# Row-half products in turns, one tile for the q of two heads, and other numbers in the planner of a linear-attention and MoE kernel

## The chip, the cores and the metric

One core of a Trainium2 chip runs the whole kernel. The metric is device time in microseconds (us), the median of the runs shown below. TensorE (PE) multiplies; its weight loads have rows of their own (PEld). VectorE (DVE) and ScalarE (ACT) do the elementwise work, GpSimd (POOL) a reduction over partitions, SyncE (SP) issues the DMAs.

## The reference

```python
def phi(x):
    proj = np.einsum('bhsd,df->bhsf', x, w_phi)
    proj = proj - np.max(np.abs(proj), axis=-1, keepdims=True)
    return np.concatenate([np.exp(proj), np.exp(-proj)], axis=-1)
q_p, k_p = (phi(q), phi(k))                      # q, k, v: 8 batches, 8 heads, 576 tokens, 64
kv = np.einsum('bhsf,bhsd->bhfd', k_p, v)        # w_phi: 64 x 128
z = np.sum(k_p, axis=2)
num = np.einsum('bhsf,bhfd->bhsd', q_p, kv)
den = np.einsum('bhsf,bhf->bhs', q_p, z)[..., None] + 1e-06
x = (num / den).transpose(0, 2, 1, 3).reshape(4608, 512)
out = ((x @ w_a) * (x @ w_b)) @ w_out            # 512 x 1536, 512 x 1536, 1536 x 512
```

## The kernel before

The heads are worked on in 32 pairs, i = 4 * batch + pr. For a pair `k_load` brings k and v of 512 of the 576 keys; the last 64 keys of two pairs share the tiles of `rest_load`: the first pair's lie in partitions 0 to 63, the second's in 64 to 127. `features` projects keys (tile pk), takes the largest absolute value (m), subtracts it (kd) and forms both exponentials (ke). `kv_add` (L288) multiplies them with v, which carries a column of ones, into the pair's sum kvps: for 512 keys in four chunks with 128 rows, and for the last 64 keys by `rest_add` with 64 rows, one pair at its own turn. `k_finish` copies kvps, transposes it (pt) and keeps the result as kvh and kvl.

On the query side `q_project` multiplies q with w_phi (tile pq, 288 tokens at a time, two heads, two halves), ACT copies the result (p), POOL finds the largest absolute value (mb), DVE subtracts it (L371), ACT forms both exponentials (qe) and `q_side` multiplies them with kv (tile pn).

Numbers are float32. Where a product is not "plain", each operand is split by `split` (L156 to L163) into a rounded high part in fp32r (ACT or DVE) and the rest (DVE), and three products of the parts stand for one of float32. The first pairs stay plain: PLAIN_K, PLAIN_Q and PLAIN_NUM are 5, PLAIN_KV is 7. A plain `q_project` (L342) loads q of two heads as one tile of 128 partitions and multiplies 64 rows at a time. The other kind loads each head's q twice, one copy over the other (four DMAs, two tiles of 128 partitions), and makes of it a tile qs that has the high part in the upper 64 rows and the rest in the lower (L355); wh and wl hold w_phi's parts in both halves, so that two products with 128 rows (L360) cover one head and one half of the tokens.

While attention runs, blocks of the first third of the MoE (`moe_block`, 512 tokens each, tiles pa, pb, po, L661 and L682) are put between its turns. When attention ends, the last of these blocks and two more passes with fewer products (L756, L861, L968) follow.

PSUM has eight banks here: two for ps_moe ("moe"), and in ps_att five for the tag "att" (pk, pq, pn) and one for "kvacc" (kvps and pt; in batch 0 these two use ps_moe).

The order on each engine is not that of the code: `plan` builds the program once, runs a list scheduler over it with a cost for each instruction (`Work`, the time in `LANDING` after which a DMA's data is taken to be there) and a count of the free buffers, and the second build is chained in that order. On an engine the earliest instruction of the code that is ready goes first.

Of the kernel before, what the change touches and what calls it, by code (L numbers as in the profile page):

```python
# [22 lines left out]
P = 128  # L23
# [8 lines left out]
REST_ADD_TURNS = (6, 7)  # L32
KV_TURNS = (7, 8)
PROJECT_TURNS = (0, 3, 3)
Q_TURNS, Q_STEP, QB, PB, Q32 = (4, 6, 10), 3, 2, 2, 2
# [8 lines left out]
PLAIN_K, PLAIN_Q, PLAIN_KV, PLAIN_NUM = 5, 5, 7, 5  # L44
# [23 lines left out]
def tile_kernel(ctx, tc, qT, km, kr, vm, vr, w_phi, w_a, w_b, w_out, out):  # L68
# [95 lines left out]

    def stack(hi_lo, src, eng_hi, eng_lo):

        copy(eng_hi, hi_lo, src)
        eng_lo.tensor_tensor(hi_lo[D:], src[D:], hi_lo[D:], op=ALU.subtract)
# [85 lines left out]
    def k_chunks(b, pr, c0, a1, a2, ps, consts, st):  # L254
# [6 lines left out]
        if c0 == 0:  # L261
            pool, tag, bufs = spare(b, ps)
            st["kv_ps", b, pr] = pool.tile([P, 2, 2 * F], F32, tag=tag, bufs=bufs, name=f"kvps_{u}")
            st["kv_left", b, pr] = NFULL + 1
        for c in range(2):
            kv_add(b, pr, [v_[:, c0 + c] for v_ in st["v", b, pr]], [e_[:, 2 * c : 2 * c + 2] for e_ in es], st)
# [14 lines left out]
    def kv_add(b, pr, vs, es, st):  # L281

        left = st["kv_left", b, pr] = st["kv_left", b, pr] - 1
        for j in range(2):
            parts = products(vs, es)
            for n_, (v_, e_) in enumerate(parts):
# [5 lines left out]
                    start=(left == NFULL and j == 0 and n_ == 0),  # L292
                    stop=(left == 0 and n_ == len(parts) - 1),
                    skip_group_check=True,
                )

    def spare(b, ps):

        return (ps_moe, "moe", 2) if b == 0 else (ps, "kvacc", 1)

    def k_finish(b, pr, a1, a2, ps, consts, st):
# [6 lines left out]
        pool, tag, bufs = spare(b, ps)  # L308
# [13 lines left out]
    def q_project(b, pr, a1, a2, ps, consts, st):  # L322
# [11 lines left out]
        if plain:  # L334
            q32 = a2.tile([P, S], F32, tag="q32", bufs=Q32, name=f"q32_{u}")
            nc.sync.dma_start(q32, qT[b, 2 * pr : 2 * pr + 2].rearrange("j d s -> (j d) s"))
            yield
            for i, tok in enumerate(toks):
                pq = [ps.tile([P, 512], F32, tag="att", name=f"pq_{u}_{j}_{i}") for j in range(2)]
# [1098 lines left out]
```

## Time and profile before

| | us |
|---|---|
| median of 3 runs | 1223.03 (1222.47 to 1224.77) |
| the profiled execution, its own time | 1223.91 |
| its span, first to last instruction | 1221.8 |
| PE busy | 1184.5 (97%), 6237 instructions |
| DVE busy | 1036.7 (85%), 1730 instructions |
| ACT busy | 740.0 (61%), 1388 instructions |
| POOL busy | 149.2 (12%) |

2.1 us of the execution lie outside its span, and the median lies 0.9 us under the profiled execution. A busy PE is an engine with a product in flight: a product of 256 columns has a row of 0.28 us, and the next one starts after about 0.12. So the rate of the engine is read from start to start, not from durations. A float32 product shows as two records. The last product of attention (L390) starts at 584.2 us of the span, the last of the first third of the MoE (L682) at 674.1.

### The profile page before, as it was taken

How to read it: one execution, taken by the hardware profiler on the slowest of the kernel's cores; microseconds unless marked ns; L12 is line 12 of the kernel's file. 1: busy time of each engine (PE TensorE's matmuls, PEld its weight loads, DVE VectorE, ACT ScalarE, POOL GpSimd, SP SyncE). 2: the span in 40 equal slices, each digit the busy share in tenths (PEclk: the TensorE clock that was granted, in tenths of full speed). 3: DMA queues.
4: the chain of work that ended last, by engine and by line, in shares of the span. 5: the costliest groups of instructions: out<-in, count | busy, mean ns of one | idle time of the engine just before them, and what ended most of it. 6: DMA issues, size and time to landing. Idle time of an engine off the chain costs nothing.

```text
span 1221.8 us, 17963 instructions
## 1 busy us (share of the span) xinstructions
PE 1184.5 (97%) x6237; PEld 981.5 (80%) x6237; DVE 1036.7 (85%) x1730; ACT 740.0 (61%) x1388; POOL 149.2 (12%) x68
## 2 busy tenths in 40 slices
PE   7997999999999999999989999999999999999998
PEld 4566888888888888888768988788877788888887
DVE  7999999998999899988576867888877687969686
ACT  5868898897888988887344533444434243534332
POOL 3232232223223213211000000000000000000000
PEclk9998999999999999999999999999999999999999
DMA  8654363455545445436762332837498634241322
GB/s 241 211 148 126 109 184 112 144 155 143 158 112 167 138 133 163 113 102 210 263 228 86 113 121 72 273 123 264 136 366 298 216 91 148 80 138 53 129 83 74
DMA packets 132922, 190.15 MB, mean 156 GB/s; under 512 B 35104, under 2 KB 64160, under 8 KB 132832
## 3 DMA queue, kind: packets, MB, share of 16 engines
q1 hardware_dynamic: 132832, 189.01, 49.4%
q8 instruction: 49, 0.80, 0.3%
q14 instruction: 41, 0.34, 0.1%
HBM read 126.73 MB, written 62.23 MB: 155 GB/s over the span
## 4 chain that ended last, share of the span: by engine, by line
PE 66%; DVE 17%; DMA 8%; issue 5%; ACT 2%; SPq 1%; POOL 0%; DVEq 0%; POOLq 0%; ACTq 0%
PE paa L756 7%; PE pba L756 7%; PE po L968 6%; PE kvps L288 6%; PE po L682 6%; PE pa L661 5%; PE pn L390 5%; PE pb L661 5%; PE poa L861 4%; PE pbc L756 3%; PE pac L756 3%; PE pk L232 2%; DMA o<-part 2%; PE poc L861 2%; PE pbb L756 2%
## 5 line engine op out<-in xcount | busy, mean ns | idle before, releaser
L370 POOL PARTITION_ALL_REDUCE mb<-p x64 | 149.0, 2372 | 408.0 <-ACT p L361 347.1
L163 DVE TENSOR_TENSOR qel<-qe,qeh 128x1152 fp32r<-128x1152 f32 x54 | 72.9, 1350 | 1.8 <-ACT qeh L156 1.5
L163 DVE TENSOR_TENSOR kel<-ke,keh 128x1024 fp32r<-128x1024 f32 x50 | 63.9, 1278 | 1.3 <-ACT keh L156 1.1
L371 DVE TENSOR_TENSOR p<-p,mb 128x576 f32<-128x576 f32 x64 | 61.3, 958 | 4.3 <-POOL mb L370 4.1
L156 ACT CAST qeh<-qe 128x1152 fp32r<-128x1152 f32 x54 | 62.8, 1163 | 0.1
L661 PE MATMUL pb<-xh,w_b_h 128*128 128x512 f32 x144 | 57.0, 396 | 3.2 <-DVE h L666 3.2
L968 PE MATMUL po<-hh,w_o_h 128*128 128x512 f32 x144 | 56.3, 393 | 3.0 <-DVE o L974 1.4
L682 PE MATMUL po<-hl,w_o_h 128*128 128x512 f32 x144 | 57.2, 397 | 1.2 <-DVE hl L163 1.1
L661 PE MATMUL pa<-xh,w_a_h 128*128 128x512 f32 x144 | 58.1, 403 | 0.0
L661 PE MATMUL pa<-xl,w_a_h 128*128 128x512 f32 x144 | 57.5, 399 | 0.0
L661 PE MATMUL pa<-xh,w_a_l 128*128 128x512 f32 x144 | 57.3, 398 | 0.0
L661 PE MATMUL pb<-xh,w_b_l 128*128 128x512 f32 x144 | 57.2, 397 | 0.0
L661 PE MATMUL pb<-xl,w_b_h 128*128 128x512 f32 x144 | 57.2, 397 | 0.0
L968 PE MATMUL po<-hl,w_o_h 128*128 128x512 f32 x144 | 56.3, 391 | 0.8 <-DVE hl L163 0.8
L682 PE MATMUL po<-hh,w_o_h 128*128 128x512 f32 x144 | 56.4, 395 | 0.5 <-ACT hh L156 0.5
L288 PE MATMUL kvps<-keh,vaug 128*65 128x256 f32 x200 | 56.1, 281 | 0.7 <-DVE kvl L318 0.7
L682 PE MATMUL po<-hh,w_o_l 128*128 128x512 f32 x144 | 56.7, 396 | 0.0
L288 PE MATMUL kvps<-kel,vaug 128*65 128x256 f32 x200 | 56.0, 280 | 0.6 <-DVE kel L163 0.6
L968 PE MATMUL po<-hh,w_o_l 128*128 128x512 f32 x144 | 56.1, 390 | 0.0
L244 ACT ACTIVATE ke<-kd 128x512 f32<-128x512 f32 x64 | 40.5, 633 | 25.4 <-DVE kd L236 25.3
L288 PE MATMUL kvps<-keh,vl 128*64 128x256 f32 x200 | 55.9, 279 | 0.0
L391 ACT COPY xn<-pn 65x288 f32<-65x288 f32 x128 | 48.8, 396 | 10.3 <-PE pn L390 9.1
(347 smaller groups left out, 3839.9 us busy)
## 6 DMA issues: line engine op xcount, KB each, us to landing
x<-xnorm SPq DMA_DIRECT2D x32, 512.0 KB
o<-part SPq DMA_DIRECT2D x61, 256.0 KB
q<-in_qT SPq DMA_DIRECT2D x108, 144.0 KB
xun<-xn SPq DMA_DIRECT2D x64, 146.2 KB
xnorm<-x SPq DMA_DIRECT2D x36, 256.0 KB
part<-o SPq DMA_DIRECT2D x18, 512.0 KB
part<-o SPq DMA_DIRECT2D x36, 256.0 KB
k<-in_km SPq DMA_DIRECT2D x32, 256.0 KB
```

The costliest lines, as they stand in the source:

```text
L156: eng.copy(dst, src)
L163: eng_lo.tensor_tensor(lo, src, hi, op=ALU.subtract)
L288: nc.tensor.matmul(st["kv_ps", b, pr][:width, j], v_[:, j, :width], e_[:, j], start=(left == NFULL and j == 0 and n_ == 0), stop=(left == ...
L370: nc.gpsimd.partition_all_reduce(mb, p32, P, bass_isa.ReduceOp.absmax)
L371: engine("q_sub", b).tensor_tensor(p32, p32, mb, op=ALU.subtract)
L390: nc.tensor.matmul(pn[: D + 1, :HALF], kv_[:, 2 * j + s, :], e_[:, s, tok], **at)
L391: nc.scalar.copy(xn[: D + 1, tok], pn[: D + 1, :HALF])
L661: nc.tensor.matmul(acc, w[:, cc * P : (cc + 1) * P], x, start=(k == 0), stop=(k == 3 * NCC - 1))
L682: nc.tensor.matmul(acc, w[:, cc * P : (cc + 1) * P], h, start=(k == 0), stop=(k == 3 * NFS[p] - 1))
L756: nc.tensor.matmul(accs[to][i], w_, x_, skip_group_check=True, **at)
L861: nc.tensor.matmul(accs[to][m], w_, x_, skip_group_check=True, **flags)
L968: nc.tensor.matmul(acc[key], w[:, cc * P : (cc + 1) * P], h[:, tok], skip_group_check=True, **n_)
```

## The change

1. `rest_add` now handles the last 64 keys of two pairs in one step. Its products stand in turns: one with rows 0 to 63 for the first pair, one with rows 64 to 127 for the second. For this two kvps tiles live at once: "kvacc" gets two banks, "att" four, and pt moves to "att" (in batch 0 to ps_moe).
2. Every `q_project` loads q of two heads as one tile (one DMA), and splits it whole (qh, ql). The products have 64 rows, in turns over the two heads: three for a head and a half where there were two with 128 rows. `stack` is gone.
3. One more pair is plain: PLAIN_K, PLAIN_Q, PLAIN_NUM 6, PLAIN_KV 8.
4. In the planner a product with 64 rows has a partner on the other half. The two are taken together, PE stays with products of the same number of rows for up to 40 places of the code, a change of rows costs 88 ns, float32 products are priced anew, the first product of a tile in "att" waits until the inputs of all of that tile's products are there, and `LANDING` has later and more times.

```diff
-REST_ADD_TURNS = (6, 7)
+REST_ADD_TURN = 6
-Q_TURNS, Q_STEP, QB, PB, Q32 = (4, 6, 10), 3, 2, 2, 2
+Q_TURNS, Q_STEP, QB, PB, Q32 = (4, 6, 10), 3, 1, 2, 2
-PLAIN_K, PLAIN_Q, PLAIN_KV, PLAIN_NUM = 5, 5, 7, 5
+PLAIN_K, PLAIN_Q, PLAIN_KV, PLAIN_NUM = 6, 6, 8, 6
-        ps = c.enter_context(tc.tile_pool(name="ps_att", bufs=5, space=PSUM))
+        ps = c.enter_context(tc.tile_pool(name="ps_att", bufs=4, space=PSUM))
...
-    def rest_add(b, pr, st):
-        rows = slice(pr % 2 * REST, (pr % 2 + 1) * REST)
-        kv_add(b, pr, [v_[rows] for v_ in st["rv", b, pr // 2]], [e_[rows] for e_ in st["re", b, pr // 2]], st)
+    def rest_add(b, g, ps, st):
+        vs, es = st["rv", b, g], st["re", b, g]
+        parts = products(vs, es)
+        first = [kv_sums(b, 2 * g + i, ps, st) for i in range(2)]
+        for j in range(2):
+            for n_, (v_, e_) in enumerate(parts):
+                width = D if n_ == 2 else D + 1
+                for i in range(2):
+                    rows, pr = slice(i * REST, (i + 1) * REST), 2 * g + i
+                    nc.tensor.matmul(
+                        st["kv_ps", b, pr][:width, j],
+                        v_[rows, j, :width],
+                        e_[rows, j],
...
+            st["kv_ps", b, pr] = ps.tile([P, 2, 2 * F], F32, tag="kvacc", bufs=2, name=f"kvps_{b}_{pr}")
...
-        pool, tag, bufs = spare(b, ps)
+        pool, tag, bufs = (ps_moe, "moe", 2) if b == 0 else (ps, "att", 4)
...
-        q32 = [a2.tile([P, S], F32, tag="q32", bufs=Q32, name=f"q32_{u}_{j}") for j in range(2)]
-        for j in range(2):
-            for i in range(2):
-                nc.sync.dma_start(q32[j][i * D : (i + 1) * D], qT[b, 2 * pr + j])
+        q32 = a2.tile([P, S], F32, tag="q32", bufs=Q32, name=f"q32_{u}")
+        nc.sync.dma_start(q32, qT[b, 2 * pr : 2 * pr + 2].rearrange("j d s -> (j d) s"))
         yield
-        qs = [a2.tile([P, S], F32R, tag="qs", bufs=QB, name=f"qs_{u}_{j}") for j in range(2)]
-        for j in range(2):
-            copy(engine("q_hi", b), qs[j], q32[j])
-            nc.vector.tensor_tensor(qs[j][D:], q32[j][D:], qs[j][D:], op=ALU.subtract)
-        for i in range(2):
+        parts = [(w2, q32)]
+        if not plain:
+            qh, ql = (a2.tile([P, S], F32R, tag=f"q{p}", bufs=QB, name=f"q{p}_{u}") for p in "hl")
+            split(qh, ql, q32, engine("q_hi", b), nc.vector)
+            parts = products((wh, wl), (qh, ql))
+        for i, tok in enumerate(toks):
+            pq = [ps.tile([P, 512], F32, tag="att", name=f"pq_{u}_{j}_{i}") for j in range(2)]
+            for n_, (w, x) in enumerate(parts):
+                for j in range(2):
+                    rows = slice(j * D, (j + 1) * D)
+                    at = dict(start=(n_ == 0), stop=(n_ == len(parts) - 1))
+                    nc.tensor.matmul(pq[j][:, :HALF], w[rows], x[rows, tok], **at)
             for j in range(2):
-                pq = ps.tile([P, 512], F32, tag="att", name=f"pq_{u}_{j}_{i}")
-                for n_, w in enumerate((wh, wl)):
-                    nc.tensor.matmul(pq[:, :HALF], w, qs[j][:, toks[i]], start=(n_ == 0), stop=(n_ == 1))
-                nc.scalar.copy(p32[j][:, toks[i]], pq[:, :HALF])
+                nc.scalar.copy(p32[j][:, tok], pq[j][:, :HALF])
...
-LANDING = {"raw": 5200.0, "w": 5000.0, "wd": 4000.0, "part": 3700.0, "x": 3300.0, "o": 3000.0}
+LANDING = {
+    "raw": 5600.0, "w": 5600.0, "wd": 4900.0, "part": 4600.0, "x": 3600.0, "o": 4700.0, "k": 3900.0, "q": 3500.0,
+    "v": 4100.0, "rk": 3700.0, "rv": 3200.0, "rb": 3900.0, "xun": 4200.0, "xnorm": 3800.0,
+}
+AHEAD_POOLS, AHEAD_BY = ("a1", "a2", "ps_att"), 0
+BESIDE, TURNED, STAY = 4.0, 88.0, 40
...
+            choice = min(beside or pairs or choice, key=lambda x: x[0][0] + STAY * (works[x[1]].rows != rows))
...
+            if w.rows != rows:
+                next_, end, rows = next_ + TURNED, end + TURNED, w.rows
```

PE, batch 5, before: the sums of the last 64 keys for its third pair. rvh, rvl are the parts of v, keh and kel those of the exponentials.

```order
L390 MATMUL pn_2_1_5084<-qeh_2_4851,kvl_1_4981 65x288 x2
L288 MATMUL kvps_2_5032<-keh_1_r,rvh_1_4727 65x256
L288 MATMUL kvps_2_5032<-kel_1_r,rvh_1_4727 65x256
L288 MATMUL kvps_2_5032<-keh_1_r,rvl_1_4728 64x256
L288 MATMUL kvps_2_5032<-keh_1_r,rvh_1_4727 65x256
L288 MATMUL kvps_2_5032<-kel_1_r,rvh_1_4727 65x256
L288 MATMUL kvps_2_5032<-keh_1_r,rvl_1_4728 64x256
L232 MATMUL pk_3_2_5107<-wkh,kh_3_4874 128x256
```

Six products stand alone between others of 128 rows; the fourth pair's six come later. PE, the same batch, after: the sums of the third and the fourth pair, and the first q products of the fourth.

```order
L277 MATMUL kvps_2_4915<-keh_1_r,rvh_1_4623 65x256
L277 MATMUL kvps_3_4976<-keh_1_r,rvh_1_4623 65x256
L277 MATMUL kvps_2_4915<-kel_1_r,rvh_1_4623 65x256
L277 MATMUL kvps_3_4976<-kel_1_r,rvh_1_4623 65x256
...
L277 MATMUL kvps_2_4915<-keh_1_r,rvl_1_4624 64x256
L277 MATMUL kvps_3_4976<-keh_1_r,rvl_1_4624 64x256
L359 MATMUL pq_3_0_0_5056<-qh_3_5052,wh 128x288
L359 MATMUL pq_3_1_0_5057<-qh_3_5052,wh 128x288
```

Twelve products stand in turns, and twelve of q follow at once. PE, the same batch, before: the q products of the fourth pair, and what stands behind them.

```order
L360 MATMUL pq_3_0_1_5176<-qs_3_0_5162,wh 128x288
L360 MATMUL pq_3_0_1_5176<-qs_3_0_5162,wl 128x288
L360 MATMUL pq_3_1_1_5180<-qs_3_1_5163,wh 128x288
L360 MATMUL pq_3_1_1_5180<-qs_3_1_5163,wl 128x288
L232 MATMUL pk_0_0_5212<-wkh,kh_0_5117 128x256
L311 MATMUL pt_2_5195<-ident,kvT_2_5150 128x65 x4
```

Four of the eight are shown; they have 128 rows, as have those around them. PE, the same batch, after: the end of the q products of the third pair, and what stands behind them.

```order
L359 MATMUL pq_2_0_1_4825<-ql_2_4812,wh 128x288
L359 MATMUL pq_2_1_1_4826<-ql_2_4812,wh 128x288
L359 MATMUL pq_2_0_1_4825<-qh_2_4811,wl 128x288
L359 MATMUL pq_2_1_1_4826<-qh_2_4811,wl 128x288
L303 MATMUL kvps_2_4915<-keh_2_0_4807,vaug_121 65x256
L303 MATMUL kvps_2_4915<-kel_2_0_4808,vaug_121 65x256
L303 MATMUL kvps_2_4915<-keh_2_0_4807,vl_2_4600 64x256
L322 MATMUL pt_1_4861<-ident,kvT_1_4799 128x65 x4
```

The transposes of the pair before, now in a bank of "att", stand three products behind the run.

## Rows read from the trace of the kernel before

**Rows 1.** The chain that ended last, shares of the span by engine.

```profile
PE 66%; DVE 17%; DMA 8%; issue 5%; ACT 2%; SPq 1%; POOL 0%; DVEq 0%; POOLq 0%; ACTq 0%
```

**Rows 2.** Busy us of each engine by stretch (x instructions), PE clock, DMA share, GB/s.

```profile
0.00:50.00 50.00, 41.86 (x173) 24.61 (x174) 41.83 (x88) 35.23 (x75) 14.85 (x11) 1.00 0.75 225
50.00:100.00 50.00, 42.84 (x198) 27.63 (x197) 46.73 (x86) 34.53 (x71) 13.03 (x6) 0.93 0.55 158
100.00:172.00 72.00, 70.05 (x417) 59.10 (x416) 71.30 (x111) 62.44 (x121) 22.52 (x9) 0.98 0.48 139
172.00:585.00 413.00, 409.77 (x2564) 358.55 (x2563) 386.36 (x598) 351.56 (x671) 98.84 (x44) 1.00 0.49 143
675.00:1222.00 547.00, 534.89 (x2528) 444.25 (x2527) 433.29 (x733) 219.15 (x379) 0.00 (x0) 1.00 0.46 154
```

**Rows 3.** What PE waited for, whole run: total us, times, longest.

```profile
PE pk L232 <- DMA k<-in_km: 5.7, 1, 5.7
PE pt L311 <- ACT kvT L306: 4.7, 5, 2.0
```

**Rows 4.** Order of time on PE around six products of 64 rows: start, us.

```profile
166.97 0.28 PE L288 MATMUL kvps<-keh,vl 128*64 128x256 f32 x1
167.18 0.33 PE L288 MATMUL kvps<-keh_r,rvh 64*65 64x256 f32 x1
167.35 0.28 PE L288 MATMUL kvps<-kel_r,rvh 64*65 64x256 f32 x1
167.46 0.28 PE L288 MATMUL kvps<-keh_r,rvl 64*64 64x256 f32 x1
...
167.81 0.28 PE L288 MATMUL kvps<-keh_r,rvl 64*64 64x256 f32 x1
168.02 0.40 PE L360 MATMUL pq<-qs,wh 128*128 128x288 f32 x1
168.26 0.30 PE L360 MATMUL pq<-qs,wl 128*128 128x288 f32 x1
...
168.79 0.29 PE L360 MATMUL pq<-qs,wl 128*128 128x288 f32 x1
```

**Rows 5.** The same view at three places with plain products of 64 rows.

```profile
20.79 0.75 PE L342 MATMUL pq<-q,w 64*128 64x288 f32 x2
...
47.56 0.76 PE L342 MATMUL pq<-q,w 64*128 64x288 f32 x4
...
60.73 0.38 PE L288 MATMUL kvps<-ke_r,rv 64*65 64x256 f32 x1
60.82 0.40 PE L342 MATMUL pq<-q,w 64*128 64x288 f32 x1
60.94 0.38 PE L288 MATMUL kvps<-ke_r,rv 64*65 64x256 f32 x1
61.06 0.40 PE L342 MATMUL pq<-q,w 64*128 64x288 f32 x1
```

**Rows 6.** Groups by line and shape: count, busy us, mean ns, idle before.

```profile
L360 PE MATMUL pq<-qs,wh 128*128 128x288 f32 x108 | 31.7, 313 | 3.6 <-DVE qs L355 1.8 <-DVE kd L236 1.6
L288 PE MATMUL kvps<-keh_r,rvh 64*65 64x256 f32 x48 | 14.5, 302 | 0.0
```

**Rows 7.** The same view, four groups of DVE and ACT.

```profile
L163 DVE TENSOR_TENSOR qel<-qe,qeh 128x1152 fp32r<-128x1152 f32 x54 | 72.9, 1350 | 1.8 <-ACT qeh L156 1.5
L163 DVE TENSOR_TENSOR kel<-ke,keh 128x1024 fp32r<-128x1024 f32 x50 | 63.9, 1278 | 1.3 <-ACT keh L156 1.1
...
L156 ACT CAST qeh<-qe 128x1152 fp32r<-128x1152 f32 x54 | 62.8, 1163 | 0.1
...
L361 ACT COPY p<-pq 128x288 f32<-128x288 f32 x108 | 36.4, 405 | 2.7 <-PE pq L360 2.5
```

**Rows 8.** Busy us of line L355 alone by stretch (DVE: qs, x instructions).

```profile
0.00:172.00 172.00, 8.97 (x12) 0.97 0.58 170
172.00:585.00 413.00, 32.09 (x42) 1.00 0.49 143
```

More of the change, by code (lines that the diff above doesn't have):

```diff
@@ L1194, in __init__ @@
         n = self.width
+        self.rows = i.get("tile_size", (P,))[0]
+        self.at = i.get("tile_position", (0,))[0]
+        self.pair_of = [x["memref"] for x in ins] if self.rows < P else None
         if self.engine == "PE":
@@ L1242, in plan @@
     place = {name: k for k, name in enumerate(names)}
+    turn = {
+        name: (place[name] - AHEAD_BY * any(homes[t][0][0] in AHEAD_POOLS for t in works[name].tiles), place[name])
+        for name in works
+    }
+    partner, before, started, due = {}, None, set(), None
+    for name in names:
+        if name in works and works[name].engine == "PE":
+            w, x = works.get(before), works[name]
+            if w and x.pair_of and w.pair_of == x.pair_of and w.at != x.at:
+                partner[before], before = name, None
+            else:
+                before = name
+    first_of = {b: a for a, b in partner.items()}
     users, first = {}, {}
@@ L1264, in plan @@
                     needs[name].add(b)
+    for t, by in users.items():
+        if homes[t][0] == ("ps_att", "att"):
+            products = [name for name in by if works[name].engine == "PE"]
+            for name in products:
+                needs[products[0]] |= {dep for dep in needs[name] if dep not in works or works[dep].engine != "PE"}
     followers, missing = {}, {}
@@ L1279, in plan, with taken, both_fit @@
     port_until, vector = 0.0, (0.0, 0.0, False)
-    tensor_end, cold = 0.0, (0.0, 0.0)
+    tensor_end, cold, rows = 0.0, (0.0, 0.0), P
+    def taken(name):
+        tiles = works[name].tiles
+        return (tiles | works[partner[name]].tiles if name in partner else tiles) - live
+    def both_fit(name):
+        other = partner.get(name)
+        if other is None:
+            return name not in first_of or first_of[name] in started
+        return missing[other] == (name in needs[other])
     def lacking(name):
         need = {}
-        for t in works[name].tiles - live:
+        for t in taken(name):
             need[homes[t][0]] = need.get(homes[t][0], 0) + 1
@@ L1289, in enter @@
         homes_taken = set()
-        for t in works[name].tiles - live:
+        for t in taken(name):
             live.add(t)
@@ L1293, in enter @@
             homes_taken.add(homes[t][0])
-        heapq.heappush(later[works[name].engine], (ready[name], place[name], name))
+        heapq.heappush(later[works[name].engine], (ready[name], turn[name], name))
         for home in homes_taken:
@@ L1300, in offer @@
         if short:
-            parked[short[0]].append((place[name], name))
+            parked[short[0]].append((turn[name], name))
         else:
@@ L1351, in plan @@
             choice = [x for x in choice if not works[x[1]].port] or choice
-        choice = min(choice)
+        if e == "PE":
+            beside = [x for x in choice if x[1] == due]
+            due = None
+            pairs = [x for x in choice if both_fit(x[1])]
+            choice = min(beside or pairs or choice, key=lambda x: x[0][0] + STAY * (works[x[1]].rows != rows))
+        else:
+            choice = min(choice)
         at_hand[e].remove(choice)
@@ L1373, in plan @@
         free[e] = now + next_
+        if name in partner and both_fit(name):
+            free[e], due = now + BESIDE, partner[name]
+        started.add(name)
         order[e].append(name)
```

49 lines of the change are left out of this document (20 added, 29 removed).

## The prediction

> **What bounds the kernel now.** I read the chain of work that ended last first: two thirds of it are PE, 17% DVE [rows 1]. Then the busy time by stretch. Three stretches differ [rows 2]. Up to 172 us DVE is nearly full (41.8 + 46.7 + 71.3 = 159.9 of 172 us) while PE is idle for 172 - 154.8 = 17.2 us. From 172 to 585 us PE is in work for 409.8 of 413 us, DVE for 386.4. From 675 us on only MoE runs, PE for 534.9 of 547. So in the first stretch DVE work sets the pace and PE has holes. In the second every product taken off PE is time, as long as no other engine takes over. The last stretch is touched by the planner's numbers alone. What PE waits for in the whole run is short: the two longest are 5.7 us for the first load and 4.7 us for the copies that stand ahead of the transposes [rows 3].
>
> Since a busy PE may still start products faster, I cost its work from start to start. Products of 256 columns with 64 rows start (167.81 - 167.46) / 3 = 0.117 us apart (two rows are left out between them), q products of 288 columns with 128 rows (168.79 - 168.26) / 4 = 0.132 us (three left out) [rows 4]. By column that is the same 0.46 ns: a product of 64 rows takes as long as one of 128.
>
> **A change of rows has a price.** In [rows 4] the last product of 128 rows starts at 166.97 and the first of 64 at 167.18: 0.21 where 0.12 is usual, so 0.09 more. The first of 64 rows takes 0.17, 0.05 more. The way out takes 0.21 again (167.81 to 168.02), 0.09 more, and the first product of 128 rows 0.24 for 0.13 (168.02 to 168.26), 0.11 more. One run of 64-row products thus costs 0.34 us beside its products. The two extra gaps of 0.05 and 0.11 go with the columns of the weights, 65 for v and 128 for w_phi; a run that begins with q products (128 columns) is therefore taken at 0.39.
>
> **Do two halves run side by side?** The trace has this only for plain float32. One plain q product, two records, takes 0.75 us from its first start to its last end; two of them on the two halves, four records, take 0.76 [rows 5]. At 60.7 us sums and q products stand on different halves at the same time, and each keeps its own spacing: 0.21 for the sums (60.73 to 60.94), 0.24 for q (60.82 to 61.06) [rows 5]. The 0.01 us is spread over two records, so I take a pair as one product plus 0.005: 0.122 for sums, 0.137 for q. The bounds for fp32r, which streams 288 columns in 0.132 instead of 0.24 us and of which the trace shows no pair, are 0.132 (perfect overlap) and 0.264 (none) for q. I stay at 0.137, since [rows 5] show no slowing.
>
> The Trainium skill speaks against part of this: in "TensorE: Matmul & The Clock Gate" (Part 3, Measured speedup vs the span model) four row tiles of 512 columns reach 3.07 times the rate of one, not 4. An estimate from that page, with the same loss for two tiles, would be 1.3 times one product for a pair, 0.172 for q and 0.152 for sums; the sum below would then end at about 1217.8. The trace differs from it so far: 0.76 against 0.75 us.
>
> **PE's work from 172 us on.** Of the 54 tiles qs 42 are made after 172 us [rows 8], so 168 of the 216 q products (108 of each of two kinds, [rows 6]) lie there and, by their place in the program, 132 of the 144 fp32r sums (48 of each of three kinds, [rows 6]), in 23 runs of six.
> - Before: 132 x 0.117 + 168 x 0.132 + 23 runs x 0.34 = 15.4 + 22.2 + 7.8 = 45.4 us.
> - After: 264 q products and 132 sums are all in turns in the changed order, 132 and 66 pairs, in 31 runs, 12 that begin with sums and 19 with q: 66 x 0.122 + 132 x 0.137 + 12 x 0.34 + 19 x 0.39 = 8.1 + 18.1 + 4.1 + 7.4 = 37.7 us.
>
> That is **-7.7 us**. The sums give 7.3 of it; the q products save 4.1 us of streaming, and the changes of rows, which q did not need before, cost 3.7 more. It lies wholly on PE in the stretch where PE has no holes. DVE loses more there than PE: each of the 42 subtractions L355 (32.1 us) is replaced by half as many of twice the partitions and the same 576 columns, at the same 0.76 us, so -16 us [rows 8]. ACT casts half as many too. Neither engine becomes the bound.
>
> **The stretch up to 172 us.** PE's own work hardly changes, counted at the same prices in both orders: fp32r sums and q products -3.7 and their runs +1.5, plain sums in eight pairs -3.4, the new plain products of the sixth and eighth pair +1.7, plain q products, of which fewer stand in turns, +2.4, and their runs +1. That is about zero, and I take zero. What changes is DVE: two subtractions qel (2 x 1.35) and two kel (2 x 1.28) go with the new plain pairs, 5.3 us [rows 7], and 12 subtractions L355 of 8.97 us become five, -5.2 us [rows 8]; the shorter ones of k and v are left out. So DVE loses about 10.5 of 160 us. PE can give back at most its holes, 17.2 less the 5.7 before the first load [rows 2, 3]: 11.5. Between 0 and -10.5 I take half, **-5 us**, because DVE is the engine that is full but part of PE's holes are waits for ACT copies ahead of the transposes (4.7 us, [rows 3]), which stay.
>
> **Banks.** "att" has four banks instead of five, and the transposes now come out of them. Between 172 and 585 us PE is out of work for only 3.2 us [rows 2], so there is little to win and something to lose; the bounds are -1 and, by the rival below, +20. I take **+1**: the planner counts the banks, and in most places products that need none of them stand behind a run.
>
> **DMA and list.** Of the q loads 81 issues on SP fall away and no queue gets longer; nobody waits for them on PE [rows 3], so zero. `rest_add` holds two kvps banks at once; behind it on PE would stand the run of q, and the price is in the bounds of the banks. The later landings shift orders in the MoE stretch, where PE is idle 12.1 us [rows 2]; I bound this by -4 and +4, a third of that, and take 0.
>
> **Sum.** -7.7 - 5 + 1 = -11.7 us. The profiled execution has a span of 1221.8, so 1210.1, and an own time of 1223.9, so 1212.2. It lies 0.9 us above the median, so I forecast **1211.3** for the median. Its own range: 5.5 more early and 4 in the list, together 1201.8, of which I go to 1203; on the other side nothing early and 4 lost in the list, 1220.3.
>
> **The rivals.**
> - *The halves do not overlap in fp32r.* Then each pair costs twice one product: 132 x 0.127 + 66 x 0.112 = 24 us more after 172 us, 1235. For it: the trace has no fp32r pair, and fp32r streams at nearly twice the rate of a plain record (0.132 against 0.24). Against it: [rows 5]. It decides from 11.7 / 198 = 0.059 us a pair, a q pair of 0.196.
> - *PE waits for the four banks: slower.* A run of twelve q products fills all four, and ACT frees each by a copy of 0.405 us [rows 7], 1.62 us for a run that PE streams in 0.84. In the changed order 17 of 33 such runs have a product that needs a bank, mostly the transposes, 0 to 0.7 us behind them, and ACT is in work for 351.6 of 413 us [rows 2], so that the copies can stand behind a cast. If a cast of 1.16 us [rows 7] has just begun when the first half's products end, two copies follow it and PE comes 0.42 (the second half) + 0.35 later, it waits 1.16 + 0.81 - 0.77 = 1.2 us; 17 times that is 20 us, the time 1230, and it is slower from 0.75 us a place. For it: a bank less with the same users and one more. Against it: the first half's copies start while the second half streams, and the waits today are short [rows 3]. The Trainium skill has the rule in "TensorEngine Tiling (Array Packing)" (Performance Considerations, PSUM Bottleneck): tiling makes TensorE faster, not the evacuation of PSUM. By that rule it would come out this way; no row of before shows a tiled run in fp32r.
> - *DVE's relief comes through whole.* Then the early part is -10.5 and the time 1205.8. For it: DVE is in work for 71.3 of 72 us from 100 us on [rows 2]. Against it: the chain of the first pairs, k load, exponentials, copy, transposes, is not DVE's alone [rows 3].
> - *The pairs are not issued as pairs.* The changed order has them in turns throughout for fp32r, so only a wait between the two could part them; this I count with the first rival.
>
> **Chances.** Forecast with its own range, the whole relief of DVE in it, 0.74; banks 0.13, a third of it still under 1220.6; no or half overlap 0.07; other waits of the new list 0.06. This kernel's measurement tells some 0.2%, 2.4 us, from no change. Faster (under 1220.6) 0.79, same (to 1225.5) 0.09, slower 0.12. The range 1203 to 1222 leaves out the upper part of the banks, the failed overlap and the far end of all gains together, about 0.2.
>
> **What will show it.** Pairs right: in order of time on PE two fp32r products of 64 rows start within 0.01 us or each keeps its half's spacing, and a run of twelve q products lasts about 0.84 us plus its 0.39. The late part right: the last product L390 starts some 12 us before 584.2, and the PE work from 172 us on shrinks by 7 to 8. The early part right: PE's idle time up to 172 us falls from 17 towards 12. Banks wrong: waits of PE for ACT copies p or of pt behind the q runs, over 0.3 us each. The forecast is wrong if q pairs take over 0.196 us, or if PE between 172 and 570 us is out of work for more than 15 us.

## The result and the profile after

The changed kernel takes **1200.87 us** (median of 4 runs, 1200.47 to 1202.95) against 1223.47 (4 runs) for the kernel before: ratio 0.9818, 95% interval 0.9801 to 0.9835. That is 22.6 us less. The forecast was 11.7 less, and its range ended at 1203. The sign was right, the size half of the truth. The profiled execution of after has a span of 1201.2 us and an own time of 1202.95.

The chain that ended last is more PE and less DVE and DMA than in [rows 1]:

```profile
PE 71%; DVE 12%; issue 6%; DMA 5%; ACT 4%; POOL 1%; SPq 1%; DVEq 0%; POOLq 0%; ACTq 0%
```

Busy time by stretch, the same stretches and columns as [rows 2]:

```profile
0.00:50.00 50.00, 38.64 (x136) 21.51 (x137) 41.59 (x84) 31.00 (x64) 13.80 (x10) 0.90 0.70 209
50.00:100.00 50.00, 48.75 (x226) 29.24 (x225) 44.47 (x87) 35.48 (x77) 15.64 (x6) 1.00 0.58 161
100.00:172.00 72.00, 72.00 (x456) 58.71 (x455) 63.51 (x107) 60.15 (x119) 19.59 (x9) 1.00 0.48 139
172.00:585.00 413.00, 411.45 (x2695) 356.50 (x2694) 369.83 (x588) 345.87 (x661) 97.77 (x44) 1.00 0.47 135
675.00:1222.00 547.00, 515.22 (x2382) 426.74 (x2380) 416.40 (x700) 208.24 (x355) 0.00 (x0) 1.00 0.45 150
```

From 100 to 172 us PE is now in work without a break, and DVE has 63.5 instead of 71.3 us. From 172 to 585 us DVE loses 16.5 us, yet PE's busy time hardly differs from [rows 2]: 411.45 and 409.77 of 413. The busy share can't tell what was won there.

The halves work side by side. A run of twelve q products in order of time on PE (start, us; x2 is one product on each half; unrounded, the second of the two starts 0.001 to 0.004 us after the first in the two runs shown):

```profile
235.05 0.39 PE L683 MATMUL po<-hl,w_o_h 128*128 128x512 f32 x1
235.28 0.40 PE L683 MATMUL po<-hh,w_o_l 128*128 128x512 f32 x1
235.61 0.40 PE L359 MATMUL pq<-qh,wh 64*128 64x288 f32 x2
235.84 0.29 PE L359 MATMUL pq<-ql,wh 64*128 64x288 f32 x2
235.97 0.29 PE L359 MATMUL pq<-qh,wl 64*128 64x288 f32 x2
...
236.37 0.29 PE L359 MATMUL pq<-qh,wl 64*128 64x288 f32 x2
236.59 0.33 PE L303 MATMUL kvps<-keh,vaug 128*65 128x256 f32 x1
236.76 0.28 PE L303 MATMUL kvps<-kel,vaug 128*65 128x256 f32 x1
```

And a run of twelve sums:

```profile
210.12 0.39 PE L662 MATMUL pb<-xl,w_b_h 128*128 128x512 f32 x1
210.44 0.33 PE L277 MATMUL kvps<-keh_r,rvh 64*65 64x256 f32 x2
210.61 0.28 PE L277 MATMUL kvps<-kel_r,rvh 64*65 64x256 f32 x2
...
211.08 0.28 PE L277 MATMUL kvps<-keh_r,rvl 64*64 64x256 f32 x2
211.29 0.50 PE L662 MATMUL pb<-xh,w_b_l 128*128 128x512 f32 x1
211.63 0.39 PE L662 MATMUL pb<-xh,w_b_h 128*128 128x512 f32 x1
```

From the second pair to the sixth the q pairs lie (236.37 - 235.84) / 4 = 0.13 us apart, the sums' (211.08 - 210.61) / 4 = 0.12; from the unrounded starts it is 0.132 and 0.117. One product alone takes the same 0.132 and 0.117 [rows 4]: a pair costs nothing beyond one of its products. The price of a run is that of [rows 4]. For q it is 0.10 in (0.33 for 0.23), 0.10 for the first pair, 0.09 out and 0.05 after it, 0.34 together; for sums 0.09 + 0.05 + 0.09 + 0.11.

The last product L390 starts at 565.99 us (584.24 before). The rows that replace L360 of [rows 6] and L355 of [rows 8], and the cast of q on ACT:

```profile
L359 PE MATMUL pq<-qh,wh 64*128 64x288 f32 x104 | 18.0, 334 | 0.4 <-ACT p L361 0.4
L163 DVE TENSOR_TENSOR ql<-q,qh 128x576 fp32r<-128x576 f32 x26 | 20.4, 785 | 4.9 <-ACT qh L156 4.9
L156 ACT CAST qh<-q 128x576 fp32r<-128x576 f32 x26 | 17.9, 688 | 0.4 <-DMA q<-in_qT 0.4
```

### Where the time went

I cut both traces at the same places in PE's work: at the 144th and at the 1008th product of 512 columns, which only MoE issues. Each gap from one start to the next is then divided into the product's own time (0.227 us for 512 columns, 0.132 for 288, 0.117 for 256), the extra at changes of rows, waits (what is left, where over 0.06 us), and small rest. In us, worked out from all records on PE:

| | 144th at | 144th to 1008th | products | changes of rows | waits | small | 1008th to last |
|---|---|---|---|---|---|---|---|
| before | 172.1 | 430.3 | 408.6 | 7.8 | 8.3 | 5.6 | 613.5 |
| after | 167.4 | 415.7 | 397.1 | 10.5 | 4.1 | 4.0 | 611.4 |
| difference | -4.7 | -14.6 | -11.5 | +2.7 | -4.3 | -1.6 | -2.1 |

How products and small rest are parted depends by about 1 us on how transposes and pairs are counted; the starts, the totals and the waits do not.

The early -4.7 and the products' -11.5 are near what the prediction had. The other 5 to 6 us of the middle were not in it: before, PE starts its next product late by 8.3 us in sum, and by another 5.6 in small gaps, in a stretch in which the busy view shows 4.4 us out of work:

```profile
172.00:602.00 430.00, 425.64 (x2631) 371.01 (x2630) 394.93 (x617) 358.03 (x684) 98.84 (x44) 1.00 0.50 147
```

A product that waits behind the one before it, and the tail of that one, still count as busy. The waits are few events: nine gaps with over 0.2 us of wait hold 5.8 of the 8.3 us. PE's own list of waits before, 172 to 585 us (us in total, times, longest), shows where to look:

```profile
PE pq L360 <- DVE qs L355: 0.9, 1, 0.9
PE pt L311 <- ACT kvT L306: 0.9, 1, 0.9
PE kvps L288 <- DVE kvl L318: 0.7, 2, 0.5
PE kvps L288 <- DVE kel L163: 0.6, 2, 0.4
```

The wait of the first line, DVE and then PE:

```profile
199.83 1.16 DVE L163 TENSOR_TENSOR kel<-ke,keh 128x1024 fp32r<-128x1024 f32 x1
201.03 1.43 DVE L355 TENSOR_TENSOR qs<-q,qs 64x576 fp32r<-64x576 f32 x2
```

```profile
200.54 0.40 PE L661 MATMUL pa<-xh,w_a_l 128*128 128x512 f32 x1
201.84 0.40 PE L360 MATMUL pq<-qs,wh 128*128 128x288 f32 x1 [0.90 <-DVE qs L355]
```

DVE is late with qs since it does kel first, and PE starts 1.30 us after its last product where 0.23 is usual. Idle time is put at 0.90, the hole is 1.07. After, the same view has only this left:

```profile
PE kvps L303 <- ACT keh L156: 1.0, 1, 1.0
PE pq L359 <- ACT p L361: 0.4, 1, 0.4
PE pa L662 <- ACT h L666: 0.2, 1, 0.2
```

Three theories could explain the closed holes: the halved casts and subtractions of q on ACT and DVE (A), the later landings in the list (B), or the gathering of bank needs on the first product (C). The experiments undo one part of the change, or make one alone in the kernel before. In the expected texts A appears as the DVE theory and as the relief of both engines, B and the planner's other numbers as the list theory. The planner's new prices of float32 products and its rule that takes pairs together were not tried apart. All ratios are to the kernel before on the same chip; medians of before were 1223.8 to 1224.7 us. Profiled executions lie up to 3 us off the medians, so a figure by segment says where, and the median how much. A bare + or - is the run's median less that of after or, for a run of the kernel before, less that of before.

### The profile page after: what moved, and what is told of

Its sections match the earlier page's. It is cut to its first block, busy times and chain, and to the rows that moved or that the text cites. A ratio compares the mean times of both kernels' runs of the same rounds, so it can differ in the third digit from the quotient of the medians.

```text
span 1201.2 us, 17915 instructions
## 1 busy us (share of the span) xinstructions
PE 1172.4 (98%) x6321; PEld 963.9 (80%) x6321; DVE 1002.1 (83%) x1695; ACT 720.8 (60%) x1355; POOL 146.8 (12%) x68
## 4 chain that ended last, share of the span: by engine, by line
PE 71%; DVE 12%; issue 6%; DMA 5%; ACT 4%; POOL 1%; SPq 1%; DVEq 0%; POOLq 0%; ACTq 0%
PE paa L757 7%; PE po L683 7%; PE po L969 7%; PE pba L757 7%; PE pn L390 6%; PE pb L662 6%; PE pa L662 6%; PE kvps L303 5%; PE pbc L757 3%; PE pac L757 3%; PE poa L862 3%; PE pk L227 3%; PE pq L359 2%; PE pab L757 2%; PE pbb L757 2%
## 5 line engine op out<-in xcount | busy, mean ns | idle before, releaser
L371 DVE TENSOR_TENSOR p<-p,mb 128x576 f32<-128x576 f32 x64 | 66.2, 1034 | 5.9 <-POOL mb L370 5.2
L163 DVE TENSOR_TENSOR kel<-ke,keh 128x1024 fp32r<-128x1024 f32 x48 | 59.3, 1236 | 7.9 <-ACT keh L156 7.9
L391 ACT COPY xn<-pn 65x288 f32<-65x288 f32 x128 | 49.0, 393 | 21.6 <-PE pn L390 21.5
```

The lines of the kernel that those rows point to most:

```text
L163: eng_lo.tensor_tensor(lo, src, hi, op=ALU.subtract)
L371: engine("q_sub", b).tensor_tensor(p32, p32, mb, op=ALU.subtract)
L391: nc.scalar.copy(xn[: D + 1, tok], pn[: D + 1, :HALF])
```

## Experiments: the parts one by one

**The sums one pair at a time.** `rest_add` as before, two runs of six products; the rest as changed.

```diff
-REST_ADD_TURN = 6
+REST_ADD_TURNS = (6, 7)
...
-    def rest_add(b, g, ps, st):
...
-                for i in range(2):
-                    rows, pr = slice(i * REST, (i + 1) * REST), 2 * g + i
+    def rest_add(b, pr, ps, st):
+        rows = slice(pr % 2 * REST, (pr % 2 + 1) * REST)
+        kv_add(b, pr, [v_[rows] for v_ in st["rv", b, pr // 2]], [e_[rows] for e_ in st["re", b, pr // 2]], ps, st)
```

> The changed kernel with the sums of the last 64 keys one pair at a time, as before; q stays in turns. By the prices of rows: sums stream 7.7 us longer and some 10 to 12 runs of 64 rows are added (3 to 4 us), so 1211 to 1213 where PE is the bound (my prices). If the waits decide instead, as they did for q, 1215 or more.

Measured 1213.43 us, ratio 0.9901 (0.9877 to 0.9925): 12.6 us of the gain are gone. Products from the 144th to the 1008th take 407.0 instead of 397.1 us (+9.9, of which 66 more sums at 0.117 are 7.7), changes of rows 12.6 instead of 10.5, and the 144th starts 4.2 us later. The waits stay small (3.0): what the sums win in the middle they win by streaming, as the price list had it.

**q as before.** The old `q_project`: 128 rows, four loads of half a tile, two casts and two half subtractions for each pair.

```diff
-Q_TURNS, Q_STEP, QB, PB, Q32 = (4, 6, 10), 3, 1, 2, 2
+Q_TURNS, Q_STEP, QB, PB, Q32 = (4, 6, 10), 3, 2, 2, 2
...
+        for j in range(2):
+            copy(engine("q_hi", b), qs[j], q32[j])
+            nc.vector.tensor_tensor(qs[j][D:], q32[j][D:], qs[j][D:], op=ALU.subtract)
```

> The changed kernel with the q products of 128 rows and the four loads of before; the sums stay in turns. By prices of rows alone: q streams 4.6 us longer, 19 runs of 64 rows fewer (6 to 7 us), so about 1199 if nothing else counts (list theory). DVE theory: 54 subtractions of 64 partitions come back, some 20 us of DVE, and with them 5 to 8 us of holes: 1204 to 1208.

Measured 1212.11 us, 0.9899 (0.9877 to 0.9921), 11.2 us slower than after and above the ranges of both theories. On PE the products cost only 4.1 us more and the changes of rows 7.2 us less, so for PE alone the old q would be the better one by 3 us. What makes it slower are waits, 14.1 instead of 4.1 us. Two of the longest entries, 172 to 602 us:

```profile
PE pt L322 <- ACT p L372: 1.5, 2, 1.0
PE pq L371 <- DVE qs L366: 1.2, 2, 1.1
```

So q's part of the change does not pay through TensorE's row halves. These lines name ACT and DVE; how much of it is their work for q is tried below, where doubling both steps of the split brings back 4.2 of these 10 us of waits. The rest, with the form of the products and the four loads in it, was not parted.

**The plain pairs as before.** `PLAIN_K, PLAIN_Q, PLAIN_KV, PLAIN_NUM = 6, 6, 8, 6` back to 5, 5, 7, 5.

```diff
-PLAIN_K, PLAIN_Q, PLAIN_KV, PLAIN_NUM = 6, 6, 8, 6
+PLAIN_K, PLAIN_Q, PLAIN_KV, PLAIN_NUM = 5, 5, 7, 5
```

> The changed kernel with the plain pairs of before (5, 5, 7, 5). DVE theory: 1204 to 1206, the 144th product of the MoE 3 to 5 us later than in the changed kernel, the rest alike, since two pairs' splits (7 us of DVE) come back where DVE is full. List theory: 1200 to 1202, since PE has 1.7 us less to do there.

Measured 1208.32 us, 0.9864 (0.9838 to 0.989): +7.5. The 144th product starts at 172.9 us, as late as before, and the middle is unchanged (416.5). So the early 4.7 us need the plain pairs; the smaller q work alone wins nothing there. They are not the plain pairs' alone: with the sums undone the 144th product stands at 171.6 us, too.

**One plain pair more.** The same line with 7, 7, 9, 7.

```diff
-PLAIN_K, PLAIN_Q, PLAIN_KV, PLAIN_NUM = 6, 6, 8, 6
+PLAIN_K, PLAIN_Q, PLAIN_KV, PLAIN_NUM = 7, 7, 9, 7
```

> The changed kernel with one more plain pair (7, 7, 9, 7). If the casts and subtractions of the first pairs still set the pace ahead of the 144th product of the MoE: 1197 to 1199. PE is in work for 72.0 of 72 us from 100 to 172 us in the changed kernel; if that bounds it now, the 1.7 us of longer products are paid: 1201 to 1204.

Measured 1203.1 us, 0.9825 (0.981 to 0.984), 2.2 more than after, the intervals overlapping. The stretch from 100 to 172 us with 5, 5, 7, 5 and with 7, 7, 9, 7 (columns as in [rows 2]):

```profile
100.00:172.00 72.00, 67.80 (x419) 56.86 (x420) 65.51 (x105) 59.27 (x112) 21.65 (x8) 0.95 0.45 125
```

```profile
100.00:172.00 72.00, 72.00 (x423) 56.89 (x420) 55.49 (x94) 53.38 (x105) 19.96 (x10) 1.00 0.45 129
```

With 5, 5, 7, 5 PE is out of work for 4.2 us and its granted clock is 0.95, worth up to another 0.05 x 72 = 3.6 us. With 7, 7, 9, 7 DVE has 8 us less than after, but PE was full already (72.00 of 72) and wins nothing: the 144th product stands at 167.3. There DVE's relief ends; what bounds the stretch from 100 us on is PE itself.

**The plain pairs alone, in the kernel before.**

```diff
-PLAIN_K, PLAIN_Q, PLAIN_KV, PLAIN_NUM = 5, 5, 7, 5
+PLAIN_K, PLAIN_Q, PLAIN_KV, PLAIN_NUM = 6, 6, 8, 6
```

> The kernel before with the new plain pairs (6, 6, 8, 6) and nothing else. By the undone experiment (1208.3 against 1200.9) the plain pairs are worth 5 to 7 us by themselves: 1216 to 1218, all of it ahead of the 144th product of the MoE. If they only help together with the turns: 1221 to 1224.

Measured 1220.34 us, 0.9962 (0.9946 to 0.9978): -4.1. The profiled execution is 3.1 us faster than this median: in it 3.4 us lie before the 144th product (168.6) and 2.9 behind the 1008th, while the middle stays at 429.9.

**The banks alone, in the kernel before.** Four banks in "att", two in "kvacc", the transposes from "att".

```diff
-        ps = c.enter_context(tc.tile_pool(name="ps_att", bufs=5, space=PSUM))
+        ps = c.enter_context(tc.tile_pool(name="ps_att", bufs=4, space=PSUM))
...
-            pool, tag, bufs = spare(b, ps)
-            st["kv_ps", b, pr] = pool.tile([P, 2, 2 * F], F32, tag=tag, bufs=bufs, name=f"kvps_{u}")
+            st["kv_ps", b, pr] = ps.tile([P, 2, 2 * F], F32, tag="kvacc", bufs=2, name=f"kvps_{u}")
...
-        return (ps_moe, "moe", 2) if b == 0 else (ps, "kvacc", 1)
+        return (ps_moe, "moe", 2) if b == 0 else (ps, "att", 4)
```

> The kernel before with the banks of the changed one alone: four for att with the transposes in them, two for kvps, all else as before. If the banks were a cost that the other parts paid for: 1226 to 1232, with PE waiting for ACT copies behind q. If two kvps banks are a gain of their own that the prediction did not see: 1217 to 1221. My +1: 1223 to 1225.

Measured 1227.37 us, 1.0032 (1.0017 to 1.0047): +2.7. Waits from the 144th to the 1008th product rise from 8.3 to 11.9 us, and PE now waits for copies of p that free banks (172 to 602 us):

```profile
PE pt L310 <- ACT p L360: 2.1, 2, 1.1
PE pq L359 <- ACT p L360: 1.0, 3, 0.4
```

The cost is there, nearly three times the term of +1 (the waits are those of a profiled execution 3.1 us above the median); in the changed kernel only 0.4 us of it is to be seen.

**The needs gathered on the first product** (theory C). The planner's rule taken out of the changed kernel.

```diff
-    for t, by in users.items():
-        if homes[t][0] == ("ps_att", "att"):
-            products = [name for name in by if works[name].engine == "PE"]
-            for name in products:
-                needs[products[0]] |= {dep for dep in needs[name] if dep not in works or works[dep].engine != "PE"}
```

> The changed kernel without the planner's rule that the first product of a tile in att waits for the inputs of all its products. If that rule closed PE's holes: 1205 to 1209, with waits inside the q, k and pn tiles. If not: 1200 to 1202.

Measured 1203.17 us, 0.9815 (0.9788 to 0.9843): +2.3 by the medians, with overlapping intervals. Waits in the middle are 3.1 us: C does not explain the closed holes.

## Experiments: the holes in the middle

**The subtraction done twice** (theory A, DVE's half). One more `ql` of the same size after the first.

```diff
             split(qh, ql, q32, engine("q_hi", b), nc.vector)
+            nc.vector.tensor_tensor(ql, q32, qh, op=ALU.subtract)
```

> The changed kernel with the subtraction that makes ql done twice, so that DVE works as long on q as before the change (26 more subtractions of 128x576, some 20 us in all); PE has the same products. If DVE's relief closed PE's holes (DVE theory): 1206 to 1210, with PE's lost time between the 144th and the 1008th product of the MoE up by 4 to 6 us and the first 144 up by 1 to 2. If the planner's new numbers closed them (list theory): 1201 to 1202.

Measured 1201.57 us, 0.9816 (0.9794 to 0.9838): no change in the time. In the profiled execution the middle is 2.1 us longer, with 5.6 us of waits instead of 4.1, and the 144th product starts 2.8 us earlier (164.6), so the two cancel. DVE's relief by itself closes at most a part of the holes.

**The cast done twice** (ACT's half; tried after the next one, which its expected text quotes).

```diff
+            copy(engine("q_hi", b), qh, q32)
             split(qh, ql, q32, engine("q_hi", b), nc.vector)
```

> The changed kernel with the cast of q on ACT done twice, the subtraction once. The subtraction twice cost 0.7 us, both twice 6.6. If ACT is the engine that counts: 1206 to 1208. If it takes both, since the casts hold up DVE and DVE holds up PE: 1201 to 1203.

Measured 1202.39 us, 0.9827 (0.9808 to 0.9846): +1.5, within the scatter. The middle is 2.3 us longer, with 5.9 us of waits, and the part behind the 1008th product 2.0 shorter.

**Both twice.**

```diff
             split(qh, ql, q32, engine("q_hi", b), nc.vector)
+            split(qh, ql, q32, engine("q_hi", b), nc.vector)
```

> The changed kernel with both steps of q's split done twice, the cast on ACT (26 x 0.68 us) and the subtraction on DVE (26 x 0.76 us): elementwise work as before, products as changed. That DVE's share alone counts has fallen with the run before (doubled subtractions: 1201.6 against 1200.9). If ACT's and DVE's relief together closed PE's holes: 1205 to 1209, with 4 us or more of waits back between the 144th and the 1008th product. If it is the form of the q products and the planner's rules: 1201 to 1203.

Measured 1207.48 us, 0.9849 (0.9825 to 0.9873): +6.6, against 0.7 and 1.5 for the halves. Waits from the 144th to the 1008th product are back at 8.3 us, the sum of before. The stretch is 6.2 us longer than in after: 4.2 of it are waits and some 1.7 changes of rows, since the planner prices the doubled work and makes another order, with 36 runs of 64-row products there instead of 31. PE's waits, 172 to 585 us:

```profile
PE kvps L303 <- ACT keh L156: 1.7, 1, 1.7
PE po L684 <- ACT hh L156: 1.2, 1, 1.2
PE pt L322 <- ACT p L362: 0.5, 1, 0.5
```

So A holds for both engines together, with two limits. The waits that come back do not stand where those of before stood, and none is for q. And only by the medians is the whole more than its halves: in the middle, waits rise by 1.6 and 1.9 us for the halves and by 4.2 for both. That slack on one engine takes up the delay of the other is not shown.

**The old landings in the changed kernel** (theory B).

```diff
-LANDING = {
-    "raw": 5600.0, "w": 5600.0, "wd": 4900.0, "part": 4600.0, "x": 3600.0, "o": 4700.0, "k": 3900.0, "q": 3500.0,
-    "v": 4100.0, "rk": 3700.0, "rv": 3200.0, "rb": 3900.0, "xun": 4200.0, "xnorm": 3800.0,
-}
+LANDING = {"raw": 5200.0, "w": 5000.0, "wd": 4000.0, "part": 3700.0, "x": 3300.0, "o": 3000.0}
```

> The changed kernel with the landing times of before in the planner, all else as changed. List theory: 1206 to 1209, the holes of the middle stretch back (4 to 6 us) and the 2 us of the MoE after it. DVE theory: 1201 to 1203, at most the 2 us that the stretch after the 1008th product had gained.

Measured 1206.61 us, 0.9855 (0.9831 to 0.9879): +5.7. The total is the list theory's, the place is not: the middle stays closed (waits 3.7). In the profiled execution, which is 2.4 us longer than that of after, the loss lies before the 144th product (+0.9) and behind the 1008th (+1.7). The intervals of this ratio and of that of both steps twice touch that of after (0.9801 to 0.9835), so these two prices are less sure than their medians look, though no single run of either is below 1204.6 and none of after above 1203.

**The new landings alone, in the kernel before.** The same table put in there.

> The kernel before with the new landing times in the planner and nothing else. Undone in the changed kernel they cost 5.7 us by the median, while the profile shows 2.4, of which 1.7 behind the 1008th product of the MoE. If they are worth that by themselves: 1218 to 1221, mostly in the MoE stretch. If they only fit the changed list: 1223 to 1226.

Measured 1217.58 us, 0.9943 (0.9926 to 0.9959): -7.1. Here waits in the middle fall from 8.3 to 4.4, and the part behind the 1008th product from 613.5 to 609.6 us, while the 144th product starts 1.7 us later. To part the two I ran the table's halves alone, both in the kernel before. **The six raised times**, which are for weights and MoE's tiles:

```diff
-LANDING = {"raw": 5200.0, "w": 5000.0, "wd": 4000.0, "part": 3700.0, "x": 3300.0, "o": 3000.0}
+LANDING = {"raw": 5600.0, "w": 5600.0, "wd": 4900.0, "part": 4600.0, "x": 3600.0, "o": 4700.0}
```

> The kernel before with the six landing times that it had raised as in the changed one (raw, w, wd, part, x, o; the last three also cover x, xun tiles of the MoE), without the eight new ones. If the MoE's own loads were planned too early: the 3.9 us behind the 1008th product come from here, 1219 to 1221, the middle stretch as before. If both stretches gain from one set alone, the sets tell which.

Measured 1223.03 us, 0.9995 (0.9981 to 1.001): nothing in sum. In the profiled execution the middle is even 4.2 us longer (waits 12.6 instead of 8.3), the part ahead of the 144th product 1.8 shorter and that behind the 1008th 2.4: another order by itself moves a stretch by as much as the holes in question. **The eight new times**, most of them for attention's loads, which until then took the planner's 2400 ns:

```diff
-LANDING = {"raw": 5200.0, "w": 5000.0, "wd": 4000.0, "part": 3700.0, "x": 3300.0, "o": 3000.0}
+LANDING = {
+    "raw": 5200.0, "w": 5000.0, "wd": 4000.0, "part": 3700.0, "x": 3300.0, "o": 3000.0, "k": 3900.0, "q": 3500.0,
+    "v": 4100.0, "rk": 3700.0, "rv": 3200.0, "rb": 3900.0, "xun": 4200.0, "xnorm": 3800.0,
+}
```

> The kernel before with the eight new landing times alone (k, q, v and their last 64 keys, rb, xun, xnorm). If loads of attention that came later than planned made PE's holes between the 144th and the 1008th product: the 3.9 us there come from here, 1219 to 1221, the MoE stretch as before.

Measured 1217.03 us, 0.9948 (0.9929 to 0.9968): -7.4, all of it. Waits in the middle are 4.1 us, as in after. PE's waits there and the busy row, 172 to 585 us:

```profile
PE pa L661 <- ACT h L665: 0.4, 1, 0.4
```

```profile
172.00:585.00 413.00, 412.45 (x2576) 361.70 (x2574) 384.72 (x602) 352.98 (x676) 100.55 (x43) 1.00 0.50 143
```

DVE is as full as before (384.7 us against 386.4) and PE no longer waits for it. The landings add no work and no transfer; they only change the order that the planner makes. Is it that loads no longer come late? DVE's waits for rb, 172 to 585 us, are these in the kernel before, in that with the six raised times, and in the changed kernel; with the eight new ones in the kernel before there is no such line:

```profile
DVE x L618 <- DMA rb<-rec: 3.4, 3, 1.9
```

```profile
DVE x L618 <- DMA rb<-rec: 4.1, 4, 2.3
```

```profile
DVE x L619 <- DMA rb<-rec: 7.1, 3, 5.5
```

The changed kernel has the eight times too, and its line is the longest of all, with PE's holes closed. Nor do the places fit. In the kernel before these waits of DVE end at 298.8, 445.6 and 516.3 us (the first is shown), while PE's two longest holes up to 585 us stand ahead of all three, at 201.84 (shown above) and 222.22:

```profile
222.22 0.46 PE L311 MATMUL pt<-ident,kvT 65*128 65x65 f32 x4 [0.88 <-ACT kvT L306]
```

```profile
298.80 0.69 DVE L618 TENSOR_TENSOR x<-x,rb 128x512 f32<-128x512 f32 x1 [1.93 <-DMA rb<-rec]
```

ACT's one wait for a load there, 0.6 us for q, ends at 205.4. So it is not shown that late loads made the holes. Shown is that the order planned with the eight times has fewer of them; why, and which of the eight does it, stays open. B holds in the kernel before, as a change of order. In the changed kernel the middle stays closed without it: the two gains are not additive.

## Experiments: the number of runs

**STAY 0.** The planner's price of a change of rows from 40 to 0, in the changed kernel.

```diff
-BESIDE, TURNED, STAY = 4.0, 88.0, 40
+BESIDE, TURNED, STAY = 4.0, 88.0, 0
```

> The changed kernel without the preference for products of the same number of rows (STAY 0): 70 runs of 64 rows instead of 56, every fp32r pair still in turns. At 0.34 us a run 14 more cost 4.8 us: 1205 to 1206. If a change of rows costs nothing beside the waits that are there anyway: 1200 to 1202.

Measured 1202.64 us, 0.9823 (0.9808 to 0.9838): +1.8. There are 70 runs instead of 56, 40 instead of 31 in the middle. Nine at 0.34 are 3.1 us, and changes of rows there cost 4.2 more (14.7 for 10.5), but the looser order gives some of it back in waits (3.15 for 4.05) and ahead of the 144th product (165.7 for 167.4).

**STAY 80.**

```diff
-BESIDE, TURNED, STAY = 4.0, 88.0, 40
+BESIDE, TURNED, STAY = 4.0, 88.0, 80
```

> The changed kernel with STAY 80 instead of 40: 51 runs of 64 rows instead of 56. Five runs fewer are 1.7 us: 1199 to 1200 if rows decide; 1201 to 1203 if products that are put off longer make waits of their own, as the 70 runs of STAY 0 cost only 1.8 us where 4.8 were expected.

Measured **1197.18 us**, 0.978 (0.9756 to 0.9804): 3.7 us faster than after by the medians, faster than both kernels. There are 51 runs, 28 instead of 31 in the middle; changes of rows there are 8.9 us, 1.6 less, where three runs at 0.34 are 1.0. Most of the rest lies ahead of the 144th product (164.4 instead of 167.4), and there the clock differs. The first 50 us of this kernel, and 40 to 45 us of it (columns as in [rows 2]; the clock is the third from the end):

```profile
0.00:50.00 50.00, 38.75 (x156) 22.45 (x156) 42.70 (x85) 31.53 (x66) 13.62 (x10) 0.97 0.72 218
40.00:45.00 5.00, 4.20 (x16) 2.05 (x15) 5.00 (x11) 3.47 (x8) 0.90 (x1) 0.81 0.69 226
```

The same 50 us of after have 0.90: 0.07 x 50 = 3.5 us at full speed. The other order of the first plain products goes with a shorter time at the lower clock. That this is the cause was not tried apart, and the intervals of the two ratios overlap.

## Why the prediction was wrong by half

By its own steps:

- **Do two halves run side by side?** Right, at the cheap end: 0.132 and 0.117 us where 0.137 and 0.122 were taken. The rival of no overlap falls. The Trainium skill's 3.07 for four row tiles ("TensorE: Matmul & The Clock Gate", Part 3, Measured speedup vs the span model), as an estimate 1.3 for a pair, is not borne out for two tiles of fp32r: the trace shows 1.00.
- **A change of rows has a price.** Right: 0.34 us for both runs shown above (0.39 was taken for one that begins with q), and +2.7 us in the middle where 3.7 was taken.
- **PE's work from 172 us on.** -7.7 predicted, -11.5 + 2.7 = -8.8 measured. The sums carry it, as said (12.6 us when undone). q was taken as about even on PE, 4.1 less streaming for 3.7 more changes. Beside paired sums it has 20 runs more (31 in the middle, 11 when undone), and the undone q shows a loss of 3 on PE.
- **The stretch up to 172 us.** -5 predicted, -4.7 measured, in part by luck: the half was a choice between two bounds, and its reason does not hold. The waits for ACT copies ahead of the transposes, which were to stay, are gone (PE's waits up to 172 us have 3.8 us of them before and none after). Of the two parts of DVE's relief the plain pairs are the one that shows (without them the 144th product is back at 172.9 us). It stops where PE has no holes left, from 100 us on.
- **Banks.** +1 predicted, +2.7 alone in the kernel before, next to nothing visible in the changed one. The rival's 20 us did not come. The rule named beside that rival ("TensorEngine Tiling (Array Packing)" of the Trainium skill, Performance Considerations, PSUM Bottleneck) is about tiled runs; only the changed kernel has them in fp32r, and PE waits 0.4 us there for copies of p. The 3.1 us of such waits with the banks alone are those of q products of 128 rows.
- **DMA and list: a term put at nothing that was not.** The loads of q at zero were not refuted. The later landings were to "shift orders in the MoE stretch", bounded by -4 and +4 and taken as 0. By themselves they are worth 7 us in the kernel before, and more than half of it lies in the middle, by the eight times that are mostly for attention's loads; the six for weights and MoE's tiles do nothing in sum. The order made with them was read in no row of before: a line of [rows 3] names what released a product, not what the planner had put ahead of it. Undone in the changed kernel the table costs 5.7 us by the medians, none of it in the middle.
- **The holes in the middle: the step that failed.** "PE is in work for 409.8 of 413 us" was taken as "no holes", so that ACT's and DVE's relief was priced at nothing there ("Neither engine becomes the bound"). From start to start there were 8.3 us of waits and 5.6 of small ones, and 5.9 us of the two are gone after, more than half of what the forecast missed. I used starts to price the products and the busy share to judge the holes; the starts would have shown both. With the relief of both engines undone the waits are 8.3 us again and the kernel is 6.6 us slower by the medians, though the waits stand at other places.

The ledger: -8.8 on PE's products and changes, -5.9 from waits and small rest, -4.7 early and -2.1 behind the 1008th product make -21.5, where -11.7 was forecast. By spans it is 1221.8 - 1201.2 = 20.6; the rest is the tail behind the last product and rounding, and the profiled execution of after is 2 us above its median. What is not settled: why the order with the new landing times has fewer holes in the kernel before; how much of the middle is the relief and how much the order made from it; the -2.1 behind the 1008th product, which is of the size of the scatter, and where exactly the old landings lose their 5.7 us in the changed kernel, since its profiled execution shows only 2.4 of them.

## What to carry to other kernels

Judge whether an engine has holes by the gaps from start to start against the product's own time, not by its busy share: of the 8.3 us of waits the busy view showed 4.4, and none of the 5.6 us of small gaps. Where a planner sets the order from modelled landing times, a change to them is a new order of everything: the waits for the loads do not bound what it is worth (-7.4 us for one half of the table, nothing in sum and 4.2 us more in the middle for the other). Expect gains that close the same holes to overlap. Undone one by one, sums, q, plain pairs, landings and the gathering cost 12.6 + 11.2 + 7.5 + 5.7 + 2.3 = 39 us, of a total of 22.6.

## What was unexpected of the hardware

Two fp32r products of 64 rows on the two row halves cost the same as one, 0.132 us for 288 columns, and start 0.001 to 0.004 us apart in the runs shown. The price of a run of 64-row products is the same 0.34 us whether its products come singly [rows 4] or in pairs. And the early stretch loses time to TensorE's clock. In after, from 35 to 45 us:

```profile
35.00:40.00 5.00, 2.36 (x6) 0.88 (x6) 5.00 (x11) 3.39 (x8) 0.00 (x0) 0.86 0.75 202
40.00:45.00 5.00, 5.00 (x10) 2.05 (x10) 5.00 (x11) 3.60 (x7) 2.38 (x1) 0.50 0.54 179
```

From 35 to 40 us PE was in work for only 2.36 us; then the granted clock is 0.50, the lower level of 1.2 GHz, and a plain q product of the same size (two records) lasts 1.32 instead of 0.75 us:

```profile
35.49 0.75 PE L359 MATMUL pq<-q,w 64*128 64x288 f32 x2 [0.53 <-ACT xn L391]
38.15 0.85 PE L359 MATMUL pq<-q,w 64*128 64x288 f32 x2 [1.91 <-DVE kd L231]
...
40.29 1.32 PE L359 MATMUL pq<-q,w 64*128 64x288 f32 x2
```

In sum this costs after up to 0.10 x 50 = 5.0 us at full speed in the stretch up to 172 us, and it cost the kernel before as much, later: 0.07 x 50 + 0.02 x 72 = 4.9 [rows 2]. So the clock does not explain the gain; it is what an early hole on PE costs besides its own length.
